# The last chunk of a gated recurrence gathered for the first expert in two one-pass parts

## The chip, the cores and the metric

The kernel runs on one core of one Trainium2 chip. The metric is device time in microseconds (us) of one execution; the profile is one execution taken by the hardware profiler. TensorE (PE) multiplies matrices, VectorE (DVE), ScalarE (ACT) and GpSimd (POOL) work on tiles, and SyncE (SP) issues DMAs.

## The reference

The program is a gated linear recurrence followed by a mixture of eight experts, one expert for each token.

```python
mag = sqrt(a_re*a_re + a_im*a_im); scale = minimum(mag, 0.999) / (mag + 1e-6)
for t in range(S):                          # B=4, H=8, S=768, D=48
    new_re = ar * S_re - ai * S_im          # ar, ai: the scaled gates of step t
    new_im = ar * S_im + ai * S_re
    S_re, S_im = new_re + k[t] outer v[t], new_im
    y[t] = q[t] @ S_re
x = y as 3072 tokens of 384
do_compute = x @ w_skip > 0                 # the others stay x
e = argmax(x @ w_gate); g = softmax(x @ w_gate)[e]
out = x + g * (maximum(x @ w1[e], 0) @ w2[e])   # w1: 8x384x1024, w2: 8x1024x384
```

## The kernel before, in words

**Tiling.** The 768 steps are cut into 6 chunks c of 128; a *unit* (c,b) is one chunk of one batch b, with all 8 heads. `unit()` runs for every unit: TensorE forms the scores `pa` (q times k, L635, 16 records in two halves), VectorE masks them into `at` (L657), and the output `py` is the sum of `at` times v (L705) and of the state `st` times q (L708). ScalarE copies `py` to `yT` (L710); TensorE multiplies `yT` with `wg` (L714), which gives `px`: the unit's 128 tokens with 384 features, and the logits of gate and skip. VectorE sums the logits (`lgs`, L719), ScalarE copies the features to `xa` (L722), and a DMA writes them to the output (L724).

**The state of late chunks.** For c = 4 and 5 (`last(c)`) the state is made without TensorE: `RX[:,0]` is the carried state `T` times the first factor, by 8 ScalarE activations, one for each head (L668); `RX[:,1]` is the same state with its halves swapped (`T2`, which a DMA brings, L641), times the second factor, on VectorE (L670); VectorE joins the two to `st` (L681). `RX`, `yT` and `T2` have one buffer each.

**Routing and gather.** `route1()` takes each late unit's logits to a one-hot of its expert (`oh`, L875), to the count of earlier tokens of that expert (`pr`, two small matmuls, L877 and L878), and in the last chunk to `ohx`, a one-hot over the 240 places of expert 0 (L889). GpSimd scatters every unit's tokens to a table `xs` in memory by indirect DMA (L778). Experts 1 to 7 read their tokens from that table. Expert 0 doesn't wait for the last chunk's scatter: `early()` (L734) reads the rows of the chunks before, and `tokens(0)` (L1002) adds the last chunk's by TensorE: `pt` = sum over the four batches of `xa` times `ohx`, and the early rows times the identity. These are float32 matmuls of 120 columns, 30 of them, which the trace shows as 60 records (two passes each). `pt` has two PSUM tiles, one for each half of the places; each is split to a rounded part `xh` (ScalarE, L1029) and a rest `xl` (VectorE, L1030).

**Experts.** Each takes 8 tiles `ph` (L1057, 9 one-pass matmuls of 240 columns each: high and low parts of tokens and weights), their ReLU on ScalarE and VectorE, and two tiles `po` (L1084 to L1086). The weights of expert 0 are split to `h` (ScalarE, L989) and `l` (VectorE, L990) beside the last units, with ScalarE's cast put right behind `yT` in its queue.

**Order.** A planner in Python writes the units, routes and weight pieces by priorities and costs, and a scheduler then sets the order on each engine; every engine takes its instructions strictly in that order. `issue_after(x)` holds an instruction back until x has its place in the queue.

Of the kernel before, what the change touches and what calls it, by code (L numbers as in the profile page):

```python
# [9 lines left out]
F32 = mybir.dt.float32  # L10
F32R = mybir.dt.float32r
BF16 = mybir.dt.bfloat16
I32 = mybir.dt.int32
AF = mybir.ActivationFunctionType
# [6 lines left out]
DM = H * D  # L21
# [91 lines left out]
class Kern:  # L113
# [530 lines left out]
    def unit(self, c, b):  # L644
# [18 lines left out]
        if c > 0:  # L663
            T = self.T[b]
            X = self.un.tile([96, 2, H, D], F32, name=f"RX_{nm}", tag="RX", bufs=1)
            if late:
                for h in range(H):
                    A.activation(X[:, 0, h], T[:, h], AF.Identity, scale=self.F[:, 0, b * H + h:b * H + h + 1])  # L668
                o.act(384, H)
                V.tensor_tensor(X[:, 1], self.T2.pop(b), Fb[:, 1].to_broadcast([96, H, D]), ALU.mult)  # L670
            else:
                with self.tc.issue_after(self.cins):
                    V.tensor_tensor(X, T.unsqueeze(1).to_broadcast([96, 2, H, D]), Fb.to_broadcast([96, 2, H, D]), ALU.mult)
# [29 lines left out]
        for hp in range(H // 2):  # L703
            for j in range(2):
                PE.matmul(py[j * 64:j * 64 + 64, hp], vt_[:, 2 * hp + j], at[:, 2 * hp + j], start=True, stop=(c == 0))  # L705
            if c > 0:
                for j in range(2):
                    PE.matmul(py[j * 64:j * 64 + 64, hp], Sb[:, 2 * hp + j], QT(2 * hp + j), start=False, stop=True)  # L708
        yT = self.un.tile([128, H // 2, C], F32, name=f"yT_{nm}", tag="yT", bufs=1)
# [10 lines left out]
        else:  # L720
            A.copy(self.lg[:, b], px[:, :, 2 * D:])
        A.copy(xa[:, 0:DM].rearrange("p (a k) -> p a k", k=2 * D), px[:, :, 0:2 * D])  # L722
        r = b * S + c * C
        nc.sync.dma_start(self.out[r:r + C], xa[:, 0:DM])  # L724
# [9 lines left out]
    def early(self):  # L734

        m = self.rt.tile([128, B * XW], F32, name="early", tag="xa", bufs=2)
        o = self.un.tile([128, H * 96], F32, name="ohx", tag="kt", bufs=1)
        nx = 2 * DM
        self.xe = m[0:TP, 0:nx].rearrange("p (t d) -> p t d", d=DM)
        self.ohx = [o[:, b * CAP:(b + 1) * CAP] for b in range(B - 1)] + [m[:, nx:nx + CAP]]  # L740
        self.early_ins = self.nc.sync.dma_start(self.xe, self.xs[0:CAP, 0:DM].rearrange("(t p) d -> p t d", p=TP)).ins

    def units(self, g):
# [3 lines left out]
        for cc in range(2):  # L747
# [5 lines left out]
            if not self.last(c):  # L753
                self.lg = self.rt.tile([128, B, H // 2, E + 1], F32, name=f"lg_{c}", tag="lg", bufs=2)
            self.xa = self.rt.tile([128, B, XW], F32, name=f"xa_{c}", tag="xa", bufs=2)
            self.nc.gpsimd.tensor_copy(self.xa[:, :, DM], self.tok[:, :, c])
            for b in range(B):
# [170 lines left out]
    def attention(self):  # L928
        with ExitStack() as ctx:
# [13 lines left out]
            self.scat = []  # L943
            self.pr_ins, self.T2, self.ain, self.QK, self.Ew, self.T, self.pa, self.W, self.ready, self.nats, self.kqt = [{} for _ in range(11)]
            self.cpos = self.gates_done = self.cons_done = self.routes_done = self.units_done = 0
# [55 lines left out]

    def tokens(self, e, xg, xp, pt_):  # L1002

# [3 lines left out]
        xl = xp.tile([128, KD, CAP], F32R, name=f"xl_{e}", tag="xl")  # L1007
        pts = [pt_.tile([128, KD, TP], F32, name=f"pt_{e}_{t}", tag="pt") for t in range(2)]
        ks = lambda k: slice(k * 128, (k + 1) * 128)
        ts = lambda t: slice(t * TP, (t + 1) * TP)  # L1010
        eye = self.ident[0:TP, 0:TP]
        if e:
            for t, pt in enumerate(pts):
                for k in range(KD):
                    with self.tc.issue_after(self.ph_ins):
                        self.pt_ins = PE.transpose(pt[:, k], xg[:, t, ks(k)], eye).ins
        else:


            pr = self.pr_ins  # L1020
            for i, (b, x) in enumerate(((0, pr[2]), (1, self.px_ins), (-1, self.px_ins), (2, pr[3]), (3, pr[3]))):
                with self.tc.issue_after(x):
                    for t, pt in enumerate(pts):
                        for k in range(KD):
                            l, r = ((self.xe[:, t, ks(k)], eye) if b < 0 else
                                    (self.xa[:, b, ks(k)], self.ohx[b][:, ts(t)]))
                            PE.matmul(pt[:, k], l, r, start=(i == 0 and k == 0), stop=True, skip_group_check=True)
        for t, pt in enumerate(pts):
            self.pins = (A.copy(xh[:, :, ts(t)], pt).ins,  # L1029
                         V.tensor_tensor(xl[:, :, ts(t)], pt, xh[:, :, ts(t)], ALU.subtract).ins)  # L1030
        return xh, xl

    def moe(self):
        nc = self.nc
        V, A, PE, G = nc.vector, nc.scalar, nc.tensor, nc.gpsimd
        with ExitStack() as ctx:
# [4 lines left out]
            got = {}  # L1041
            xh, xl = self.tokens(0, None, xp, pt_)
            for e in range(E):
# [32 lines left out]
                if e + 1 < E:  # L1076
                    xh, xl = self.tokens(e + 1, got[e + 1], xp, pt_)
                for t in range(2):
# [228 lines left out]
```

## Time and profile before

| | before |
|---|---|
| median of 3 runs | 519.48 us (519.21 to 523.06) |
| profiled execution: time, span | 520.63 us, 518.9 us |
| TensorE busy, mean granted clock | 415.0 us (80%), 0.891 |
| VectorE busy | 406.9 us (78%) |
| ScalarE busy | 316.3 us (61%) |
| GpSimd busy | 100.8 us (19%) |
| moved by DMA | 88.64 MB, 173 GB/s of memory traffic |

Busy shares are means over stages. The stages here are the chunks of the recurrence, up to about 365 us, and the experts, from the first `ph` on. In the page's picture of 40 slices TensorE's digits are mixed in the first 24 slices and 8 or 9 in the rest, so a change has to be read from the stage that it touches. [...]

### The profile page before, as it was taken

The numbers are of one execution on the slowest core, as the hardware profiler recorded it, in microseconds if no ns is written. First come the engines' busy times: TensorE is split into PE (matmuls) and PEld (weight loads), VectorE is DVE, ScalarE is ACT, GpSimd is POOL, SyncE is SP. The second block draws the span as 40 slices with busy tenths as digits, with TensorE's granted clock in tenths as the row PEclk, the third lists the DMA queues.
The fourth block names the chain that finished last, engine by engine and source line by source line (L and its number), as shares of the span: only waits on it lengthen the run. The fifth ranks groups of instructions, "written<-read, shape, count | busy, mean of one in ns | idle before, by whom it ended". The sixth has DMA issues, their size and how long they took to land. (4 is left out here: it accounts for less than half of the span.)

```text
span 518.9 us, 10077 instructions
## 1 busy us (share of the span) xinstructions
PE 415.0 (80%) x3221; PEld 360.2 (69%) x3221; DVE 406.9 (78%) x1111; ACT 316.3 (61%) x746; POOL 100.8 (19%) x174
## 2 busy tenths in 40 slices
PE   0336545499899313999999999998999999999993
PEld 0224323379777202688787888997899999999993
DVE  4999897989999999688878956888569668766730
ACT  5778777655557665568878665674266546554520
POOL 4002011111123454001000151321311111211111
PEclk9976666589999655699999999998999999999998
DMA  5557876589889887877755348764788668666300
GB/s 95 114 111 169 198 182 141 134 190 215 215 194 239 196 209 170 187 159 150 174 127 137 78 106 237 177 194 123 242 227 246 218 230 275 188 200 222 116 21 27
DMA packets 165218, 88.64 MB, mean 171 GB/s; under 512 B 138939, under 2 KB 158860, under 8 KB 165159
## 3 DMA queue, kind: packets, MB, share of 16 engines
q1 hardware_dynamic: 158135, 72.09, 55.2%
q0 software_dynamic: 5936, 15.65, 10.9%
q8 instruction: 28, 0.46, 0.4%
q10 hardware_dynamic: 1088, 0.20, 0.2%
q14 instruction: 31, 0.25, 0.2%
HBM read 63.19 MB, written 26.58 MB: 173 GB/s over the span
## 5 line engine op out<-in xcount | busy, mean ns | idle before, releaser
L496 PE MATMUL sw<-ws,ident 128*128 128x384 f32 x84 | 44.4, 665 | 34.5 <-ACT ws L482 34.5
L413 DVE TENSOR_TENSOR X<-W,ain 128x192 f32<-128x192 f32 x192 | 68.0, 354 | 3.5 <-ACT ain L339 0.2
L990 DVE TENSOR_TENSOR l<-r,h 128x768 fp32r<-128x768 f32 (+1 forms) x56 | 59.5, 1066 | 12.4 <-ACT h L989 12.2
L1059 ACT ACTIVATE hh<-ph 128x240 fp32r<-128x240 f32 x64 | 23.6, 374 | 58.1 <-PE ph L1057 58.0
L989 ACT CAST h<-r 128x768 fp32r<-128x768 f32 (+1 forms) x56 | 51.6, 928 | 5.3 <-DMA r<-in_moe_w_dram 4.9
L496 PEld LDWEIGHTS sw<-ws,ident 128*128 128x128 f32 x84 | 19.3, 254 | 47.0 <-ACT ws L482 37.3
L422 DVE TENSOR_TENSOR W<-X 128x96 f32<-128x96 f32 x192 | 49.0, 255 | 3.6
L1057 PE MATMUL ph<-xh,l 128*128 128x240 f32 x192 | 51.1, 275 | 0.0
L1057 PE MATMUL ph<-xh,h 128*128 128x240 f32 x192 | 49.7, 274 | 0.6 <-issue 0.6
L1057 PE MATMUL ph<-xl,h 128*128 128x240 f32 x192 | 49.3, 276 | 0.0
L578 PE MATMUL tp<-ident,iw 128*96 128x128 f32 x128 | 24.1, 339 | 29.5 <-DVE iw L514 24.9
L585 ACT COPY qk<-tp 96x256 f32<-96x256 f32 x128 | 39.8, 369 | 8.6 <-PE tp L578 8.3
L1084 PE MATMUL po<-h,hh 128*120 128x384 f32 x128 | 43.3, 338 | 0.0
L657 DVE TENSOR_TENSOR at<-pa,mask 128x512 f32<-128x512 f32 x48 | 32.5, 684 | 13.6 <-PE pa L635 11.5
L1085 PE MATMUL po<-l,hh 128*120 128x384 f32 x128 | 43.1, 337 | 0.0
L578 PEld LDWEIGHTS tp<-ident,iw 128*96 128x96 f32 x128 | 18.4, 158 | 34.0 <-issue 10.3
L705 PE MATMUL py<-at,vt 128*64 128x128 f32 x384 | 41.3, 287 | 0.0
L778 POOL DMA_INDIRECT xs<-xa,sl x24 | 28.6, 1193 | 64.2 <-DVE sl L845 19.9
L1086 PE MATMUL po<-h,hl 128*120 128x384 f32 x128 | 40.9, 341 | 0.0
L1060 DVE SCALAR_TENSOR_TENSOR hl<-ph,hh 128x240 fp32r<-128x240 f32 x64 | 25.6, 404 | 16.5 <-ACT hh L1059 16.0
L1090 POOL DMA_INDIRECT out_dram<-og,idx x16 | 19.3, 1209 | 87.5 <-DVE og L1089 49.2
L1057 PEld LDWEIGHTS ph<-xh,l 128*128 128x128 f32 x192 | 36.3, 189 | 0.0
(232 smaller groups left out, 1096.7 us busy)
## 6 DMA issues: line engine op xcount, KB each, us to landing
r<-in_moe_w_dram SPq DMA_DIRECT2D x24, 512.0 KB, 5.1
r<-in_moe_w_dram SPq DMA_DIRECT2D x32, 384.0 KB, 3.4
nat<-kq SPq DMA_DIRECT2D x8, 768.0 KB, 6.1
kq<-nw POOLq DMA_DIRECT2D x24, 192.0 KB, 3.7
kq<-iw POOLq DMA_DIRECT2D x24, 192.0 KB, 3.0
vt<-in_v_dram SPq DMA_DIRECT2D x24, 192.0 KB, 3.6
out_dram<-xa SPq DMA_DIRECT2D x24, 192.0 KB, 3.5
ain<-in_a_im_dram SPq DMA_DIRECT2D x90, 48.0 KB, 2.5
```

The source lines that it names most:

```text
L413: V.tensor_tensor(X, prev.unsqueeze(1).to_broadcast([128, 2, 2, D]), windows(ain[:, j]), ALU.mult)
L422: self.cins = V.tensor_tensor(W[:, j, ::-1], X[:, :, 0], X[:, :, 1], ALU.add).ins
L496: nc.tensor.matmul(sw, self.ident, ws[:, :, c], start=(c == 0), stop=(c == 1))
L578: nc.tensor.transpose(tp[:, jj], src[:, s * 4 + jj], self.ident)
L585: nc.scalar.copy(o, tp[:, :, :, cc].rearrange("p j s b -> p b s j"))
L705: PE.matmul(py[j * 64:j * 64 + 64, hp], vt_[:, 2 * hp + j], at[:, 2 * hp + j], start=True, stop=(c == 0))
L989: nc.scalar.copy(hi[:, ks], raw)
L990: nc.vector.tensor_tensor(lo[:, ks], raw, hi[:, ks], ALU.subtract)
L1057: pe = PE.matmul(ph, w[:, k, js], x[:, k], start=(n == 0), stop=(n == len(terms) - 1))
L1084: PE.matmul(po, hh[:, j, sl], w2h[:, j], start=(j == 0), stop=False)
L1085: PE.matmul(po, hh[:, j, sl], w2l[:, j], start=False, stop=False)
L1086: pe = PE.matmul(po, hl[:, j, sl], w2h[:, j], start=False, stop=(j == NF - 1))
```

## The change

For units of the last two chunks the 8 activations of `RX` now stand behind the previous unit's `yT` in ScalarE's queue. In the last chunk every unit's tokens are also written as a rounded part `hi` (ScalarE, 128x384, tile `xah`) and a rest `lo` = `xa` - `hi` (GpSimd, tile `xal`). The gather for expert 0 goes by thirds of the features, one PSUM bank for each (the third bank from the ring of `ph`): 24 one-pass matmuls of 240 columns (4 batches, 3 thirds, two parts), and 6 float32 matmuls of 120 columns for the early rows. Their places in TensorE's queue change, and the copies to `xh` and `xl` go by thirds: ScalarE, VectorE, ScalarE, and three subtractions on VectorE.

```diff
--- before.py
+++ after.py
@@ -664,8 +664,9 @@
             T = self.T[b]
             X = self.un.tile([96, 2, H, D], F32, name=f"RX_{nm}", tag="RX", bufs=1)
             if late:
-                for h in range(H):
-                    A.activation(X[:, 0, h], T[:, h], AF.Identity, scale=self.F[:, 0, b * H + h:b * H + h + 1])
+                with self.tc.issue_after(self.yT_ins):
+                    for h in range(H):
+                        A.activation(X[:, 0, h], T[:, h], AF.Identity, scale=self.F[:, 0, b * H + h:b * H + h + 1])
                 o.act(384, H)
                 V.tensor_tensor(X[:, 1], self.T2.pop(b), Fb[:, 1].to_broadcast([96, H, D]), ALU.mult)
             else:
@@ -705,7 +706,8 @@
                 PE.matmul(py[j * 64:j * 64 + 64, hp], vt_[:, 2 * hp + j], at[:, 2 * hp + j], start=True, stop=(c == 0))
             if c > 0:
                 for j in range(2):
-                    PE.matmul(py[j * 64:j * 64 + 64, hp], Sb[:, 2 * hp + j], QT(2 * hp + j), start=False, stop=True)
+                    self.py_ins[b] = PE.matmul(py[j * 64:j * 64 + 64, hp], Sb[:, 2 * hp + j], QT(2 * hp + j),
+                                               start=False, stop=True).ins
         yT = self.un.tile([128, H // 2, C], F32, name=f"yT_{nm}", tag="yT", bufs=1)
         self.yT_ins = A.copy(yT.rearrange("p a (k t) -> p a k t", k=2),
                              py.rearrange("p a (k t) -> p a k t", k=2)[:, :, :, ::-1]).ins
@@ -719,7 +721,13 @@
             V.tensor_reduce(lg, px[:, :, 2 * D:].rearrange("p h e -> p e h"), AX.X, ALU.add)
         else:
             A.copy(self.lg[:, b], px[:, :, 2 * D:])
+        if c == NCH - 1:
+            hi, lo = [t[:, b] for t in self.parts]
+            A.copy(hi.rearrange("p (a k) -> p a k", k=2 * D), px[:, :, 0:2 * D])
         A.copy(xa[:, 0:DM].rearrange("p (a k) -> p a k", k=2 * D), px[:, :, 0:2 * D])
+        if c == NCH - 1:
+            nc.gpsimd.tensor_tensor(lo, xa[:, 0:DM], hi, ALU.subtract)
+            o.act(384)
         r = b * S + c * C
         nc.sync.dma_start(self.out[r:r + C], xa[:, 0:DM])
         self.lg_t = o.act(1024, 3, o.pe(3000 if c else 2000))
@@ -734,10 +742,10 @@
     def early(self):
 
         m = self.rt.tile([128, B * XW], F32, name="early", tag="xa", bufs=2)
-        o = self.un.tile([128, H * 96], F32, name="ohx", tag="kt", bufs=1)
+        o = self.un.tile([128, B, CAP], F32R, name="ohx", tag="qkT")
         nx = 2 * DM
         self.xe = m[0:TP, 0:nx].rearrange("p (t d) -> p t d", d=DM)
-        self.ohx = [o[:, b * CAP:(b + 1) * CAP] for b in range(B - 1)] + [m[:, nx:nx + CAP]]
+        self.ohx = [o[:, b] for b in range(B)]
         self.early_ins = self.nc.sync.dma_start(self.xe, self.xs[0:CAP, 0:DM].rearrange("(t p) d -> p t d", p=TP)).ins
 
     def units(self, g):
@@ -753,6 +761,8 @@
             if not self.last(c):
                 self.lg = self.rt.tile([128, B, H // 2, E + 1], F32, name=f"lg_{c}", tag="lg", bufs=2)
             self.xa = self.rt.tile([128, B, XW], F32, name=f"xa_{c}", tag="xa", bufs=2)
+            if c == NCH - 1:
+                self.parts = [self.un.tile([128, B, DM], F32R, name=f"xa{k}", tag="nat") for k in "hl"]
             self.nc.gpsimd.tensor_copy(self.xa[:, :, DM], self.tok[:, :, c])
             for b in range(B):
 
@@ -999,35 +1009,43 @@
         self.fetch_ins = ld.ins
         return xg
 
-    def tokens(self, e, xg, xp, pt_):
+    def tokens(self, e, xg, xp, pt_, ph_):
 
         nc = self.nc
         V, A, PE = nc.vector, nc.scalar, nc.tensor
         xh = xp.tile([128, KD, CAP], F32R, name=f"xh_{e}", tag="xh")
         xl = xp.tile([128, KD, CAP], F32R, name=f"xl_{e}", tag="xl")
-        pts = [pt_.tile([128, KD, TP], F32, name=f"pt_{e}_{t}", tag="pt") for t in range(2)]
         ks = lambda k: slice(k * 128, (k + 1) * 128)
         ts = lambda t: slice(t * TP, (t + 1) * TP)
         eye = self.ident[0:TP, 0:TP]
         if e:
+            pts = [pt_.tile([128, KD, TP], F32, name=f"pt_{e}_{t}", tag="pt") for t in range(2)]
             for t, pt in enumerate(pts):
                 for k in range(KD):
                     with self.tc.issue_after(self.ph_ins):
                         self.pt_ins = PE.transpose(pt[:, k], xg[:, t, ks(k)], eye).ins
-        else:
-
-
-            pr = self.pr_ins
-            for i, (b, x) in enumerate(((0, pr[2]), (1, self.px_ins), (-1, self.px_ins), (2, pr[3]), (3, pr[3]))):
-                with self.tc.issue_after(x):
-                    for t, pt in enumerate(pts):
-                        for k in range(KD):
-                            l, r = ((self.xe[:, t, ks(k)], eye) if b < 0 else
-                                    (self.xa[:, b, ks(k)], self.ohx[b][:, ts(t)]))
-                            PE.matmul(pt[:, k], l, r, start=(i == 0 and k == 0), stop=True, skip_group_check=True)
-        for t, pt in enumerate(pts):
-            self.pins = (A.copy(xh[:, :, ts(t)], pt).ins,
-                         V.tensor_tensor(xl[:, :, ts(t)], pt, xh[:, :, ts(t)], ALU.subtract).ins)
+            for t, pt in enumerate(pts):
+                self.pins = (A.copy(xh[:, :, ts(t)], pt).ins,
+                             V.tensor_tensor(xl[:, :, ts(t)], pt, xh[:, :, ts(t)], ALU.subtract).ins)
+            return xh, xl
+
+        pts = [p.tile([128, CAP], F32, name=f"pt_{e}_{k}", tag=tag)
+               for k, (p, tag) in enumerate(((pt_, "pt"), (pt_, "pt"), (ph_, "ph")))]
+        px, pr = self.px_ins, self.pr_ins
+        for i, (b, x) in enumerate(((0, self.py_ins[2]), (1, px), (2, px), (-1, pr[3]), (3, pr[3]))):
+            with self.tc.issue_after(x):
+                for k, pt in enumerate(pts):
+                    if b < 0:
+                        for t in range(2):
+                            PE.matmul(pt[:, ts(t)], self.xe[:, t, ks(k)], eye, start=False, stop=True, skip_group_check=True)
+                        continue
+                    for n, xa in enumerate(self.parts):
+                        PE.matmul(pt, xa[:, b, ks(k)], self.ohx[b], start=(i + n == 0), stop=True, skip_group_check=True)
+        A.copy(xh[:, 0], pts[0])
+        V.tensor_copy(xh[:, 1], pts[1])
+        hi = A.copy(xh[:, 2], pts[2]).ins
+        for k, pt in enumerate(pts):
+            self.pins = hi, V.tensor_tensor(xl[:, k], pt, xh[:, k], ALU.subtract).ins
         return xh, xl
 
     def moe(self):
...
```

Up to about 325 us all queues are the same in both kernels, and from the first `ph` on they have the same order of work. Between these points three places matter. In the names the first number is the batch b, and the last a running number.

ScalarE's queue at units (5,0) to (5,2), before:

```order
L668 ACTIVATE RX_2_4328<-T_2_4008,F_4130 96x48 x4
L710 COPY yT_0_4196<-py_0_4179 128x512
L989 CAST h_0_4041<-r_0_2_4150 128x768
L668 ACTIVATE RX_2_4328<-T_2_4008,F_4130 96x48 x4
L881 ACTIVATE m_3_4314<-m_3_4314 128x8
L722 COPY xa_4145<-px_0_4198 128x384
L668 ACTIVATE RX_3_4413<-T_3_4100,F_4130 96x48 x8
L710 COPY yT_1_4283<-py_1_4266 128x512
```

and now:

```order
L712 COPY yT_0_4198<-py_0_4181 128x512
L999 CAST h_0_4041<-r_0_2_4152 128x768
L669 ACTIVATE RX_1_4245<-T_1_3923,F_4130 96x48 x8
L726 CAST xah<-px_0_4200 128x384
L727 COPY xa_4145<-px_0_4200 128x384
L891 ACTIVATE m_0_4407<-m_0_4407 128x8
L712 COPY yT_1_4287<-py_1_4270 128x512
L999 CAST h_0_4041<-r_0_4_4216 128x768
L669 ACTIVATE RX_2_4334<-T_2_4008,F_4130 96x48 x8
L726 CAST xah<-px_1_4289 128x384
L727 COPY xa_4145<-px_1_4289 128x384
L891 ACTIVATE m_1_4470<-m_1_4470 128x8
```

The activations of one unit's `RX` stood ahead of, around or (for `RX_3`) all in front of a `yT`; now all 8 stand behind the previous unit's `yT` and the weight cast, and the two copies of `px` behind them.

TensorE's queue where chunk 4 ends, from the last half of `py` of (4,3) in the first fence and from `pa` of (5,1) in the second; before:

```order
L705 MATMUL py_3_4102<-at_3_4038,vt_164 64x128 x2
L708 MATMUL py_3_4102<-qk_0_2167,st_166 64x128 x2
L705 MATMUL py_3_4102<-at_3_4038,vt_164 64x128 x2
L708 MATMUL py_3_4102<-qk_0_2167,st_166 64x128 x2
L877 LDWEIGHTS tri
L877 MATMUL pr_1_4140<-oh_1_4062,tri 128x8
L878 LDWEIGHTS ones
L878 MATMUL pr_1_4140<-ohs,ones 128x8
L635 MATMUL pa_1_0_4165<-qk_1_2168 128x128 x4
L635 MATMUL pa_1_1_4166<-qk_1_2168 128x128 x4
```

and now:

```order
L635 MATMUL pa_1_0_4167<-qk_1_2168 128x128 x4
L716 MATMUL px_2_4029<-wg,yT_2_4027 128x105 x4
L706 MATMUL py_3_4102<-at_3_4038,vt_164 64x128 x2
L635 MATMUL pa_1_1_4168<-qk_1_2168 128x128 x4
L709 MATMUL py_3_4102<-qk_0_2167,st_166 64x128 x2
L706 MATMUL py_3_4102<-at_3_4038,vt_164 64x128 x2
L709 MATMUL py_3_4102<-qk_0_2167,st_166 64x128 x2
L706 MATMUL py_3_4102<-at_3_4038,vt_164 64x128 x2
L709 MATMUL py_3_4102<-qk_0_2167,st_166 64x128 x2
L706 MATMUL py_3_4102<-at_3_4038,vt_164 64x128 x2
L709 MATMUL py_3_4102<-qk_0_2167,st_166 64x128 x2
```

Both halves of `pa` of (5,1) moved from behind `py` of (4,3) to places ahead of its state products (L708, now L709).

TensorE's queue at the end of the last chunk, from the `pr` of batch 2, before:

```order
L878 MATMUL pr_2_4503<-ohs,ones 128x8
L1027 MATMUL pt_0_4592<-ohx,xa_4145 128x120 x3
L1027 MATMUL pt_1_4593<-ohx,xa_4145 128x120 x3
L714 MATMUL px_3_4443<-wg,yT_3_4441 128x105 x4
L1027 MATMUL pt_0_4592<-ohx,xa_4145 128x120 x3
L1027 MATMUL pt_1_4593<-ohx,xa_4145 128x120 x3
L1027 MATMUL pt_0_4592<-ident,early 128x120 x3
L1027 MATMUL pt_1_4593<-ident,early 128x120 x3
L877 LDWEIGHTS tri
L877 MATMUL pr_3_4532<-oh_3_4520,tri 128x8
L878 LDWEIGHTS ones
L878 MATMUL pr_3_4532<-ohs,ones 128x8
```

and now, the last 4 of the 14 products that stand between `px_3` and `pr_3`, and what follows:

```order
L1043 MATMUL pt_1_4603<-ohx,xah 128x240
L1043 MATMUL pt_1_4603<-ohx,xal 128x240
L1043 MATMUL pt_2_4604<-ohx,xah 128x240
L1043 MATMUL pt_2_4604<-ohx,xal 128x240
L887 LDWEIGHTS tri
L887 MATMUL pr_3_4542<-oh_3_4530,tri 128x8
L888 LDWEIGHTS ones
L888 MATMUL pr_3_4542<-ohs,ones 128x8
L1040 MATMUL pt_0_4602<-ident,early 128x120 x2
L1040 MATMUL pt_1_4603<-ident,early 128x120 x2
L1040 MATMUL pt_2_4604<-ident,early 128x120 x2
L1043 MATMUL pt_0_4602<-ohx,xah 128x240
```

Before, batch 0 stood ahead of `px_3`, batch 1 and the early rows between `px_3` and `pr_3`, batches 2 and 3 behind. Now no product of the gather stands ahead of `px_3` (but 4 of batch 0 behind `py_2`), 14 short products stand between, and 12 records of early rows and 6 products of batch 3 behind.

## Rows read from the trace of the kernel before

**Rows 1.** Busy time by window: length, busy per engine (instructions), PEclk, DMA share, GB/s
```profile
350.00:355.00 5.00, 4.35 (x54) 3.91 (x54) 5.00 (x26) 2.46 (x11) 1.26 (x2) 1.00 0.61 187
355.00:360.00 5.00, 3.80 (x36) 3.61 (x37) 4.94 (x31) 2.66 (x8) 0.97 (x1) 0.76 0.37 87
375.00:380.00 5.00, 5.00 (x41) 5.00 (x40) 1.49 (x4) 2.09 (x5) 0.00 (x0) 1.00 0.75 179
400.00:440.00 40.00, 40.00 (x298) 40.00 (x296) 28.98 (x47) 22.53 (x42) 6.77 (x8) 1.00 0.75 242
```

**Rows 2.** ScalarE timeline, 343 to 366 us: start, duration, instruction, idle before and releaser
```profile
343.83 0.56 ACT L710 COPY yT<-py 128x512 f32<-128x512 f32 x1
...
348.60 0.56 ACT L710 COPY yT<-py 128x512 f32<-128x512 f32 x1
349.07 0.83 ACT L989 CAST h<-r 128x768 fp32r<-128x768 f32 x1
349.80 1.01 ACT L668 ACTIVATE RX<-T,F 96x48 f32<-96x48 f32 x4
...
353.95 1.91 ACT L668 ACTIVATE RX<-T,F 96x48 f32<-96x48 f32 x8
355.77 0.56 ACT L710 COPY yT<-py 128x512 f32<-128x512 f32 x1
...
361.09 0.59 ACT L710 COPY yT<-py 128x512 f32<-128x512 f32 x1 [1.81 <-PE py L708]
...
364.88 0.59 ACT L710 COPY yT<-py 128x512 f32<-128x512 f32 x1 [0.47 <-PE py L708]
```

**Rows 3.** TensorE timeline, 355 to 365 us, same columns
```profile
355.45 0.17 PE L877 MATMUL pr<-oh,tri 128*128 128x8 bf16 x1 [1.09 <-DVE oh L875]
...
356.39 1.14 PE L714 MATMUL px<-wg,yT 128*128 128x105 f32 x8 [0.75 <-ACT yT L710]
...
357.79 0.65 PE L708 MATMUL py<-qk,st 96*64 96x128 f32 x4
...
360.35 0.65 PE L708 MATMUL py<-qk,st 96*64 96x128 f32 x4
...
363.06 0.39 PE L708 MATMUL py<-qk,st 96*64 96x128 f32 x4
...
364.39 0.39 PE L708 MATMUL py<-qk,st 96*64 96x128 f32 x4
```

**Rows 4.** TensorE timeline at 342.6 us, the scores of one unit
```profile
342.61 2.03 PE L635 MATMUL pa<-qk 96*128 96x128 f32 x16
```

**Rows 5.** VectorE timeline, 349 to 371 us, same columns
```profile
349.86 0.55 DVE L670 TENSOR_TENSOR RX<-T,F 96x384 f32<-96x384 f32 x1 [2.01 <-DMA T<-T]
...
356.30 0.60 DVE L681 SCALAR_TENSOR_TENSOR st<-RX,sg 96x384 f32<-96x384 f32 x1
...
368.71 0.23 DVE L875 SCALAR_TENSOR_TENSOR oh<-iota,m 128x8 bf16<-128x8 f32 x1
...
370.80 0.34 DVE L889 TENSOR_SCALAR early<-iotac,m 128x240 f32<-128x240 bf16 x1
```

**Rows 6.** TensorE timeline, 365 to 376 us, end of recurrence to first expert
```profile
365.33 1.58 PE L1027 MATMUL pt<-ohx,xa 128*128 128x120 f32 x12
366.74 1.04 PE L714 MATMUL px<-wg,yT 128*128 128x105 f32 x8
...
371.79 1.50 PE L1027 MATMUL pt<-early,xa 128*128 128x120 f32 x12
373.88 0.35 PE L1057 MATMUL ph<-xh,h 128*128 128x240 f32 x1 [0.60 <-issue]
...
375.98 1.17 PE L1057 MATMUL ph<-xl,h 128*128 128x240 f32 x9
```

**Rows 7.** GpSimd by line: shapes, count, busy and mean ns, idle before
```profile
L199 POOL CAST iotac<-ii 128x240 bf16<-128x240 int32 x1 | 0.4, 372 | 0.0
...
L201 POOL MEMSET zrow<- 128x386 f32 x1 | 0.4, 410 | 0.0
```

More of the change, by code (lines that the diff above doesn't have):

```diff
@@ L943, in attention @@
             self.scat = []
-            self.pr_ins, self.T2, self.ain, self.QK, self.Ew, self.T, self.pa, self.W, self.ready, self.nats, self.kqt = [{} for _ in range(11)]
+            self.pr_ins, self.py_ins, self.T2, self.ain, self.QK, self.Ew, self.T, self.pa, self.W, self.ready, self.nats, self.kqt = [{} for _ in range(12)]
             self.cpos = self.gates_done = self.cons_done = self.routes_done = self.units_done = 0
@@ L1041, in moe @@
             got = {}
-            xh, xl = self.tokens(0, None, xp, pt_)
+            xh, xl = self.tokens(0, None, xp, pt_, ph_)
             for e in range(E):
@@ L1076, in moe @@
                 if e + 1 < E:
-                    xh, xl = self.tokens(e + 1, got[e + 1], xp, pt_)
+                    xh, xl = self.tokens(e + 1, got[e + 1], xp, pt_, ph_)
                 for t in range(2):
```

## The prediction

> **What bounds the kernel now.** I read the busy time by windows first, to see which stage is limited by what. In the first expert and in the middle of the experts TensorE is busy 5.00 of 5.00 and 40.00 of 40.00 us at a granted clock of 1.00 [rows 1]. Whatever moves the first `ph` (373.88 us, [rows 6]) therefore moves the end by as much, and nothing that the other engines do behind it counts. At 350 to 360 us it is otherwise: TensorE is busy 4.35 and 3.80 of 5.00, VectorE 5.00 and 4.94, and the clock falls to 0.76 in the second window [rows 1]. So the question is what sets the time from chunk 4's end to the first `ph`.
>
> The second view is the timeline of ScalarE and TensorE in that stretch. The five `yT` from (4,3) to (5,3) start at 343.83, 348.60, 355.77, 361.09 and 364.88 us [rows 2]: steps of 4.77, 7.17, 5.32 and 3.79 us, 21.05 in all. The third is late because the 8 activations of `RX_3` stood in front of it, 1.91 us from 353.95 [rows 2]. [...] From the last `yT` to the first `ph` 9.00 us pass (364.88 to 373.88): 12 records of batch 0 stand ahead of `px_3` and the others around and behind `pr_3` [rows 6].
>
> **The change, part by part.**
>
> *Scores ahead of `py`.* The 16 records of `pa` of (5,1) now stand in front of (4,3)'s state products. They take (2.03 - 0.28) / 15 x 16 = 1.87 us [rows 4], 0.28 being about one record's length. Before, they started when `py` of (4,3) was done, at 342.61, and that unit's `yT` waited for ScalarE until 343.83 [rows 2, 4]. Now `py` ends at 342.61 + 1.87 = 344.48 and `yT` starts 0.1 later, at 344.6: +0.8 us. If TensorE comes to this point earlier, it is 0; that is the lower bound.
>
> *The activations behind `yT`.* This makes the last chunk one serial loop, `yT`, weight cast, `RX`, `st`, state products, `yT`. Its steps: `yT` to cast 0.47 (348.60 to 349.07), cast to `RX` 0.73 (349.07 to 349.80), 8 activations 1.91 [rows 2]; `st` 0.60 [rows 5]; the state part of `py` at full clock 1.72 (363.06 to 364.39 + 0.39), and 0.10 from its end to `yT` (364.78 to 364.88) [rows 2, 3]. The sum is 5.53. Two handovers, `RX` to `st` and `st` to `py`, are in no row; the nearest is that 0.10 from TensorE to ScalarE, the lower bound is 0, and where VectorE is busy they can be longer. I take 0.10 each, so 5.73 us for a round, and four rounds 22.9 us against 21.05. The last `yT` starts at 344.6 + 22.9 = 367.5 us, 2.6 later than before.
>
> What lies beside the loop: the other half of the state, which waited 2.01 us for the DMA of `T` [rows 5], has a round of 5.73 us in place of some 4; the two copies of `px` to `hi` and `xa`, each no longer than a `yT` of more columns (0.59, [rows 2]), end some 4.3 us behind `yT` and leave ScalarE over 1 us before the next. If that cover were gone, the second copy's 0.5 us would be added to a round. VectorE worked 9.94 us for the about two units of 350 to 360 us [rows 1], some 5 of 5.73 us for a round, so it can delay `st` by some tenths; that is in the upper bound, 5.9 us.
>
> *The gather.* A 240-column product should come every 0.112 us, like those of `ph` ((1.17 - 0.28) / 8, [rows 6]), and a record of 120 columns every 0.111 ((1.50 - 0.28) / 11, [rows 6]). So 60 records become 24 + 12 = 36, and TensorE has 24 x 0.111 = 2.7 us less to do. Only what stands between the last `yT` and the first `ph` counts. From the start Y of that `yT`: `px_3` starts at Y + 0.62 (355.77 to 356.39, [rows 2, 3]), takes 1.04 [rows 6] and ends at Y + 1.7. From there to the end of `oh` it is 1.16 us (367.78 to 368.94, [rows 5, 6]), so `pr_3` could go at Y + 2.9; the 14 products in front of it take 1.57 us and end at Y + 3.2. Then 12 records of early rows (1.33) to Y + 4.6, and 6 products of batch 3 (0.67) to Y + 5.3. The one-hot of batch 3 takes 0.34 [rows 5] and a few small steps behind `pr_3`, and is there by Y + 4.2. Before, 0.59 us passed from the gather's end (371.79 + 1.50) to the first `ph`, for the copy to `xh`; now the first third's copy starts four products before the gather ends, and 0.2 of it is left. First `ph`: Y + 5.5. That is 3.5 us less than 9.00.
>
> *The subtraction on GpSimd.* No row shows one. `zrow`'s fill of 128x386 takes 0.41 us, and a conversion of 128x240 takes 0.37 [rows 7], which for 384 columns and two inputs is 0.37 x 1.6 x 2 = 1.2; I take 1.2, since it has two inputs. For batch 3 `xa` ends at about Y + 2.7 and `lo` is first used at Y + 4.7, so 2.0 us are covered and this costs nothing; one of 3 us would cost 1. [...] The scatter of batch 3 stands behind the subtraction on GpSimd's queue and moves with it; only expert 1 waits for that, some 10 us later.
>
> **The sum.** First `ph` at 367.5 + 5.5 = 373.0 us against 373.88: -0.9 us at full clock. The bounds: a round of 5.53 and no +0.8 gives 343.83 + 22.1 + 5.5 = 371.4, -2.4; a round of 5.9 gives 373.7, -0.2. To this comes the clock. One `py` at half clock cost 361.00 - 357.79 = 3.21 against 1.72 us, +1.5 [rows 3]. Before, it fell when TensorE had waited 1.09 + 0.75 us within 2 us. In the new rounds of (5,2) and (5,3) there are no scores left to fill: `py`, `px`, `pr` and four products make some 3.5 us of a round of 5.73, and 2.2 us are waits for `yT` and `st`. I expect the clock to fall once more, for one `py`: -0.9 + 1.5 = +0.6.
>
> The sum stands against the profiled execution, 520.63 us with a span of 518.9, which is 1.15 above the median of 519.48. I put the difference on the median: 520.1 us.
>
> **Rivals.**
> *Full clock (chance 0.2).* No `py` falls into a slow stretch, because the waits are spread in pieces and TensorE has work between them. Against it: before, smaller waits were enough [rows 3]. -0.9: 518.6 us.
> *Two slow rounds, the slower side (0.27).* [...] -0.9 + 3.0 = +2.1: 521.6 us. It decides as soon as the clock does not come back in (5,2)'s `py`, as it did before. For it: both waits return each round. Against it: in the profile the clock came back after one `py`. [...] If the half clock also held through the tail (3.6 us of records from `px_3`'s end), it would be +5.7: 525.2 us; I give that 0.05 of the 0.27.
> *A late part (0.07).* `lo` over 2.0 us, or the weight cast waiting for its DMA with all 8 activations now behind that cast on ScalarE. A wait of 1 us on top of the forecast: 521.1 us.
> *The loop does not form (0.06).* The queue says that `RX` is behind `yT`, but if its cost was hidden before and stays hidden, rounds keep their 21.05 us: 344.6 + 21.05 + 5.5 = 371.2, -2.7 and 516.8 us. Against it is the sum of 5.53 us, which has no slack in it.
> The forecast, one slow `py`, has the remaining 0.4.
>
> **The numbers.** The predicted time is 520.1 us. The range goes from 517.2 (full clock with a round between 5.53 and 5.73) to 523.0 us (two slow rounds with a round of 5.9 and a late part of 0.7); it leaves out the loop that doesn't form and the half clock through the tail. A measurement of this kernel can tell about 1%, 5.2 us, from no change. Of the cases only the half clock through the tail is beyond that, 0.05, and a little for what I have not seen on either side: faster 0.03, same 0.91, slower 0.06.
>
> **What would show it.** In the profile after: steps between the `yT` of chunk 5 of 5.6 to 5.9 us, and one about 1.5 longer; `RX` starting 1.2 us behind each `yT`; VectorE's `st` right behind the eighth activation. 14 products at 0.11 us between `px_3` and `pr_3`, and a first `ph` 5.5 us behind the last `yT`, at 373 to 375 us. `xal` at 0.4 to 1.2 us, with TensorE not waiting for it. The window of (5,2) with a granted clock below 1.00. I am wrong if a one-pass product of the gather takes longer than one of `ph`, if `st` waits for VectorE's other work, or if the clock stays at either level through all of the last two units.

## The result, and the profile after

The changed kernel is slower: 522.54 us median of 14 runs (519.77 to 524.92) against 516.27 for the kernel before in as many runs beside it (513.65 to 523.06); the ratio is 1.0113, with a 95% interval of 1.0082 to 1.0144. Some executions fall in a slower state; ratios are of the others alone, medians and ranges of all, so the two differ a little. The forecast time of 520.1 us and its range hold the median. The forecast difference, +0.6 us, does not hold: the measured one is +5.8 us by the ratio (1.13% of 516.27) and +6.3 by the medians, over the 1% to which I gave a chance of 0.06. The three runs of before that the forecast was put on (519.21 to 523.06) lie above ten of the eleven later ones.

Where the time went is read from one stretch, from the start of the `yT` of (4,0) to the first `ph`. In front of it the queues are the same but for a few instructions, yet the starts differ: over the 13 profiles of this study that `yT` starts between 318.1 and 325.4 us, with granted clocks of 0.82 to 0.97 at 200 to 250 us. Behind it TensorE is busy all the time (40.00 of 40 us at 400 to 440 us in both): from the first `ph` to the start of the last `po` it is 136.26 us before and 136.33 after. In the stretch it is 49.13 us before and 55.88 after, +6.75: chunk 4 takes 1.39 more, the four rounds of chunk 5 take 27.29 against 21.05, and the tail, from the `yT` of (5,3) to the first `ph`, 8.12 against 9.00.

ScalarE's timeline of the changed kernel, which answers to [rows 2] (start, duration, instruction, idle before):

```profile
341.95 0.59 ACT L712 COPY yT<-py 128x512 f32<-128x512 f32 x1 [0.94 <-PE py L709]
...
347.74 0.58 ACT L712 COPY yT<-py 128x512 f32<-128x512 f32 x1 [2.20 <-PE py L709]
...
353.50 0.58 ACT L712 COPY yT<-py 128x512 f32<-128x512 f32 x1 [1.78 <-PE py L709]
...
360.55 0.59 ACT L712 COPY yT<-py 128x512 f32<-128x512 f32 x1 [3.04 <-PE py L709]
...
361.77 1.91 ACT L669 ACTIVATE RX<-T,F 96x48 f32<-96x48 f32 x8
...
369.24 0.58 ACT L712 COPY yT<-py 128x512 f32<-128x512 f32 x1 [3.47 <-PE py L709]
```

Rounds of 5.79, 5.76, 7.05 and 8.69 us; every `yT` now waits for TensorE, none for an `RX`. TensorE's timeline, which answers to [rows 3, 6]:

```profile
354.13 1.14 PE L716 MATMUL px<-wg,yT 128*128 128x105 f32 x8 [0.60 <-ACT yT L712]
...
357.73 0.44 PE L709 MATMUL py<-qk,st 96*64 96x128 f32 x4 [2.08 <-DVE st L682]
...
359.38 0.65 PE L706 MATMUL py<-at,vt 128*64 128x128 f32 x4
...
365.89 0.69 PE L709 MATMUL py<-qk,st 96*64 96x128 f32 x4 [2.78 <-DVE st L682]
...
368.50 0.64 PE L709 MATMUL py<-qk,st 96*64 96x128 f32 x4
...
372.59 0.41 PE L1043 MATMUL pt<-ohx,xah 128*128 128x240 f32 x1
372.81 0.41 PE L1043 MATMUL pt<-ohx,xal 128*128 128x240 f32 x1
...
374.85 1.83 PE L1040 MATMUL pt<-ident,early 120*128 120x120 f32 x12
...
377.36 0.38 PE L1075 MATMUL ph<-xh,h 128*128 128x240 f32 x1
```

In (5,2) TensorE waits 0.60 us for `yT` and 2.08 for `st`, in (5,3) 2.78 for `st`; four records of `py` then take 0.65 us, as in the slow `py` of before [rows 3]. The products of the gather come every 0.21 us, at half clock (0.50 granted at 370 to 375 us), until the clock comes back in the early rows. The windows, which answer to [rows 1] and have the same columns (start and end, length, busy time of PE, PEld, DVE, ACT and POOL, granted clock, DMA share, GB/s):

```profile
355.00:360.00 5.00, 2.92 (x33) 2.57 (x33) 3.88 (x21) 2.52 (x11) 0.12 (x1) 0.83 0.63 165
360.00:365.00 5.00, 3.10 (x24) 2.35 (x20) 3.24 (x12) 3.32 (x11) 1.99 (x3) 0.83 0.07 25
365.00:370.00 5.00, 3.52 (x31) 3.10 (x31) 3.04 (x17) 1.36 (x4) 1.90 (x2) 0.52 0.72 212
370.00:375.00 5.00, 5.00 (x25) 4.92 (x26) 2.59 (x15) 0.97 (x3) 1.85 (x2) 0.50 0.78 299
375.00:380.00 5.00, 5.00 (x41) 4.81 (x42) 2.44 (x13) 1.14 (x4) 1.00 (x1) 0.96 0.10 25
400.00:440.00 40.00, 40.00 (x298) 39.99 (x297) 29.59 (x47) 22.01 (x40) 7.59 (x7) 1.00 0.73 230
```

TensorE is busy 2.92 and 3.10 of 5 us in the windows in which the clock begins to fall. Windows of 2 us show that it falls twice:

```profile
356.00:358.00 2.00, 0.28 (x5) 0.28 (x7) 2.00 (x12) 1.51 (x6) 0.00 (x0) 1.00 0.22 25
358.00:360.00 2.00, 2.00 (x26) 2.00 (x24) 0.88 (x7) 0.00 (x0) 0.00 (x0) 0.58 0.89 270
...
362.00:364.00 2.00, 1.10 (x11) 0.76 (x10) 1.97 (x5) 1.68 (x8) 1.01 (x2) 1.00 0.14 49
364.00:366.00 2.00, 0.11 (x2) 0.11 (x4) 1.93 (x11) 0.97 (x3) 1.11 (x2) 0.79 0.00 0
366.00:368.00 2.00, 2.00 (x20) 2.00 (x22) 1.43 (x6) 0.00 (x0) 0.91 (x1) 0.50 0.69 216
```

It falls behind a window with 0.28 of 2 us busy, is back at 1.00 at 362 to 364 us, and falls again around one with 0.11 busy; then it stays at 0.50 through `py` of (5,3), `px` and the 14 products. The experts run at 1.00 as before (400 to 440 us). VectorE and GpSimd beside the wait for the second `st`, which answers to [rows 5, 7]:

```profile
361.69 0.15 DVE L897 SCALAR_TENSOR_TENSOR m<-oh,pr 128x1 f32<-128x1 bf16 x1 [2.78 <-PE pr L888]
...
361.84 1.23 DVE L903 TENSOR_TENSOR ohs<-ohs,oh 128x8 bf16<-128x8 bf16 x1
...
363.51 0.96 DVE L1000 TENSOR_TENSOR l<-r,h 128x768 fp32r<-128x768 f32 x1
...
365.22 0.61 DVE L682 SCALAR_TENSOR_TENSOR st<-RX,sg 96x384 f32<-96x384 f32 x1
...
365.94 1.01 DVE L885 SCALAR_TENSOR_TENSOR oh<-iota,m 128x8 bf16<-128x8 f32 x1
```

```profile
362.17 0.88 POOL L729 TENSOR_TENSOR xal<-xa,xah 128x384 fp32r<-128x384 f32 x1
...
365.88 1.03 POOL L729 TENSOR_TENSOR xal<-xa,xah 128x384 fp32r<-128x384 f32 x1
```

`ohs`, 8 columns, takes 1.23 us and ends with GpSimd's subtraction at 363.05; `oh` takes 1.01 and ends with the next one. `RX` was ready at 363.68 (361.77 + 1.91), but `st` comes at 365.22, behind batch 1's route and the weights' `l` in VectorE's queue. VectorE itself had stood idle for 2.78 us until the `pr` of batch 1 came (361.40), which stands behind the slow `py` of (5,2) and four products of the gather in TensorE's queue: part of TensorE's wait for `st` goes back to its own slow work.

### The profile page after: what moved, and what is told of

Its sections match the earlier page's. It is cut to its first block, busy times and chain, and to the rows that moved or that the text cites. A ratio compares the mean times of both kernels' runs of the same rounds, so it can differ in the third digit from the quotient of the medians.

```text
span 522.0 us, 10028 instructions
## 1 busy us (share of the span) xinstructions
PE 415.7 (80%) x3197; PEld 359.0 (69%) x3197; DVE 410.8 (79%) x1113; ACT 316.5 (61%) x750; POOL 102.2 (20%) x178
## 5 line engine op out<-in xcount | busy, mean ns | idle before, releaser
L788 POOL DMA_INDIRECT xs<-xa,sl x24 | 26.6, 1108 | 65.9 <-DVE sl L855 20.0
L635 PE MATMUL pa<-qk 96*128 96x128 f32 x256 | 35.5, 286 | 3.3 <-DVE at L657 2.9
L635 PEld LDWEIGHTS pa<-qk 96*128 96x128 f32 x256 | 31.4, 194 | 7.5 <-DVE at L657 4.1
```

The source lines that it names most:

```text
L635: nc.tensor.matmul(pa[h // 4][:, h % 4], KT(h), QT(h), start=True, stop=True)
```

## The experiments

Stretch and parts in us, each from one profile; the ratio is to the kernel before, in runs beside it.

| kernel | (4,0) to (4,3) | rounds of chunk 5 | tail | stretch | ratio (95%) |
|---|---|---|---|---|---|
| before | 19.08 | 4.77, 7.17, 5.32, 3.79 | 9.00 | 49.13 | |
| before, again | 19.31 | 4.77, 6.79, 6.36, 5.50 | 9.00 | 51.73 | |
| changed | 20.47 | 5.79, 5.76, 7.05, 8.69 | 8.12 | 55.88 | 1.0113 (1.0082 to 1.0144) |
| changed, again | 20.47 | 5.78, 5.75, 6.99, 7.41 | 5.64 | 52.04 | 1.0107 (1.0039 to 1.0175) |
| hold alone | 20.47 | 5.78, 5.76, 7.18, 7.49 | 9.56 | 56.24 | 1.0140 (1.0080 to 1.0199) |
| gather alone | 19.25 | 4.78, 6.99, 5.73, 3.79 | 8.00 | 48.54 | 1.0034 (0.9996 to 1.0073) |
| changed, `lo` on VectorE | 20.46 | 5.79, 5.75, 7.22, 7.73 | 7.70 | 54.65 | 1.0134 (1.0075 to 1.0193) |
| gather, `lo` on VectorE | 19.24 | 4.77, 7.05, 6.37, 3.96 | 6.47 | 47.86 | 0.9989 (0.9947 to 1.0031) |
| changed, waits filled | 20.46 | 5.79, 5.75, 6.31, 6.36 | 5.53 | 50.20 | 1.0060 (1.0025 to 1.0095) |
| changed, cast behind `RX` | 20.47 | 5.75, 6.24, 6.78, 6.51 | 5.53 | 51.28 | 1.0034 (0.9995 to 1.0073) |
| hold two back | 18.08 | 4.82, 5.36, 5.49, 3.77 | 8.75 | 46.27 | 0.9991 (0.9951 to 1.0030) |
| two back, gather | 18.70 | 4.53, 6.04, 5.04, 3.81 | 6.43 | 44.55 | 0.9994 (0.9957 to 1.0031) |
| the same, casts behind ReLU | 18.38 | 4.55, 5.64, 5.05, 3.81 | 6.44 | 43.87 | 0.9950 (0.9924 to 0.9976) |

**The two halves of the change.** Hold alone, in the kernel before:

```diff
-                for h in range(H):
-                    A.activation(X[:, 0, h], T[:, h], ...)
+                with self.tc.issue_after(self.yT_ins):
+                    for h in range(H):
+                        A.activation(X[:, 0, h], T[:, h], ...)
```

> The kernel before with one edit only: the RX activations of late units held behind the previous unit's yT. Theory L: the loop forms, rounds of about 5.8 us and two slower ones at half clock, the last yT at 368 to 370 us, and the old gather of 9 us behind it, longer at half clock: first ph at 377 to 381 us, 520 to 524 us in all (before 516.3). Rival G: holding is harmless, within 1.5 us of the kernel before.

Measured: ratio 1.0140; stretch 56.24. The time of the changed kernel is there without any of the gather, and so are the waits for `st` (1.68 and 0.84 us) and the half clock:

```profile
350.00:355.00 5.00, 2.72 (x32) 2.11 (x30) 4.51 (x21) 3.60 (x12) 0.59 (x1) 0.92 0.66 165
355.00:360.00 5.00, 4.41 (x36) 3.99 (x35) 2.38 (x15) 1.89 (x5) 0.97 (x1) 0.50 0.20 67
360.00:365.00 5.00, 4.16 (x34) 3.57 (x35) 2.38 (x14) 1.79 (x8) 1.24 (x1) 0.50 0.53 173
```

The gather alone is the changed kernel with these lines taken back.

> The changed kernel with the RX activations given back their old freedom in ScalarE's queue (no holding behind yT); the two-part gather, GpSimd's subtraction and the new batch places stay. Theory L (the loop): holding RX behind yT makes chunk 5 a serial loop of 5.8 us a round and starves TensorE of work, which brings the half clock; the gather itself is a gain. Then the last yT should start near 365 us again (before 364.88, changed 369.24) and the first ph some 5.5 to 6.5 us behind it, at about 371 us: 2 to 3.5 us under the kernel before, about 513 to 514.5 us against its 516.3. Rival G (the gather's own parts): GpSimd's subtraction holds VectorE up and the gather products in front of pr delay the routes; then this kernel stays near the changed one, 520 us or more, with the last yT after 367 us.

Measured: 1.0034 (0.9996 to 1.0073): not slow as the changed kernel, but not the gain that I expected either. Its last `yT` starts where it should (362.25 in a profile that began 3.0 us earlier), and its tail is 8.00, not 5.5 to 6.5. VectorE, GpSimd and TensorE in that tail:

```profile
362.61 1.77 DVE L898 TENSOR_SCALAR ohx<-iotac,m 128x240 fp32r<-128x240 bf16 x1
...
367.10 1.55 DVE L902 TENSOR_TENSOR ohs<-ohs,oh 128x8 bf16<-128x8 bf16 x1
```

```profile
363.20 1.03 POOL L728 TENSOR_TENSOR xal<-xa,xah 128x384 fp32r<-128x384 f32 x1
...
367.75 0.88 POOL L728 TENSOR_TENSOR xal<-xa,xah 128x384 fp32r<-128x384 f32 x1
```

```profile
366.64 0.17 PE L886 MATMUL pr<-oh,tri 128*128 128x8 bf16 x1 [0.59 <-DVE m L916]
...
369.12 0.57 PE L1042 MATMUL pt<-ohx,xah 128*128 128x240 f32 x3 [0.85 <-DVE m L914]
```

A one-hot of 240 columns takes 1.77 us and `ohs` 1.55, where they take 0.33 and 0.15 elsewhere; each ends within 0.2 us of a subtraction's end (364.23 and 368.63). Both begin some 0.6 us ahead of the subtraction's recorded start, beside the scatter that GpSimd issues before it; but beside such an issue alone, in the kernel before, the same one-hot takes 0.33 (358.68, issue from 358.55 to 359.52) and `ohs` 0.15 (365.69, issue from 365.39 to 366.40). TensorE waits 0.59 and 0.85 us for that chain. Both theories were half right here.

**The subtraction on VectorE**, first in the changed kernel, then in the gather alone:

```diff
-            nc.gpsimd.tensor_tensor(lo, xa[:, 0:DM], hi, ALU.subtract)
+            V.tensor_tensor(lo, xa[:, 0:DM], hi, ALU.subtract)
```

> The changed kernel with the rest lo = xa - hi made by VectorE in place of GpSimd; all else is as changed. In the changed kernel's trace four VectorE instructions beside GpSimd's subtractions took 0.59, 1.23, 1.01 and 0.75 us where they take 0.15 to 0.23 elsewhere. Theory L: they cost about 1 us on the path to st of unit (5,3) and little else, so this kernel is 0 to 1.5 us faster than the changed one (521 to 522.5 us), with the same rounds of 5.8 us. Rival G: the stalls are the cause, and it falls to 518 us or less.

Measured: 1.0134 against 1.0113: no difference is shown. `st` of (5,3) came sooner, 7.73 in place of 8.69, but the clock was 0.50 from 360 to 375 us, so little was left of it.

> Both edits: RX not held, and lo made by VectorE. Theory L: like the gather alone, 512.5 to 514.5 us, at most 1 us faster than with GpSimd's subtraction, since VectorE has four subtractions of some 0.5 us more. Rival G: only this one is faster than the kernel before, and the gather alone is not.

Measured: 0.9989; the tail 6.47 where GpSimd's subtraction had 8.00. In the changed kernel with `lo` on VectorE a subtraction takes 0.54 to 0.56 us, and with none on GpSimd `ohs` takes 0.15 to 0.16, `oh` 0.21 to 0.22 and `ohx` 0.34 us. The expected gain of some 3 us over before would be a ratio of 0.994, just outside the interval's edge (0.9947): it is not there.

**The clock.** TensorE gets work to do in the waits of (5,2) and (5,3), without use. If the clock falls because TensorE waits there, it should stay at 1.00 now and the stretch be shorter in spite of the work; if the fall has another cause, it should be 0.50 again and the stretch no shorter.

```diff
+            if c == NCH - 1 and b > 1 and hp == 0:
+                for j in 7 * (0, 1):
+                    PE.matmul(py[j * 64:j * 64 + 64, hp], vt_[:, 2 * hp + j], at[:, 2 * hp + j], start=True, stop=True)
             for j in range(2):
                 PE.matmul(py[j * 64:j * 64 + 64, hp], ...
```

> The changed kernel with work added: in units (5,2) and (5,3) the first two products of py are written seven times more before they are written for good, 14 float32 products (28 records of 0.055 us, some 1.6 us) in front of the products that wait for st. The outputs are the same. [...]

Measured: with work added the kernel is not slower than the changed one but rather faster, 1.0060 against 1.0113 with intervals that overlap a little; the stretch is 50.20. Windows, and TensorE in (5,2):

```profile
350.00:355.00 5.00, 3.68 (x51) 3.27 (x52) 4.89 (x24) 4.09 (x13) 0.03 (x1) 1.00 0.63 155
355.00:360.00 5.00, 4.95 (x70) 4.40 (x66) 3.60 (x19) 3.29 (x11) 1.95 (x3) 1.00 0.16 59
360.00:365.00 5.00, 3.58 (x46) 3.22 (x45) 3.87 (x22) 1.57 (x5) 2.73 (x3) 1.00 0.67 206
365.00:370.00 5.00, 5.00 (x46) 4.78 (x45) 4.01 (x22) 1.51 (x5) 2.04 (x3) 1.00 0.89 328
```

```profile
351.81 1.75 PE L707 MATMUL py<-at,vt 128*64 128x128 f32 x28
353.39 0.39 PE L709 MATMUL py<-at,vt 128*64 128x128 f32 x4
354.56 0.44 PE L712 MATMUL py<-qk,st 96*64 96x128 f32 x4 [0.78 <-DVE st L682]
```

28 added records in 1.75 us leave 0.78 of the wait; the clock stays at 1.00 in this profile, and the tail is 5.53 us, with the same queue behind `px_3` that took 8.12. The rounds at full clock are 6.3 us and not 5.73: `st` is still late behind VectorE's queue. (The profile is of this kernel's shortest execution, 514.37 us where the median is 519.02; its stretch began at 318.11 us, the earliest of all 13.)

**The cast out of the loop**: the weight cast is pinned behind the last `RX` activation, not behind `yT`.

```diff
...
-                    for x in self.pins if e else (self.yT_ins, self.at_ins):
+                    for x in self.pins if e else (self.rx_ins, self.at_ins):
```

> The changed kernel with one move: the weight cast of a unit stands behind the RX activations on ScalarE, not between yT and RX; TensorE's queue is the same but for one place of one pr. Theory L: the cast is a link of the loop, 0.73 us of each round, so the first two rounds of chunk 5 take 5.0 to 5.1 us in place of 5.79 and 5.76, and the stretch from yT of (4,0) to the first ph is about 3 us shorter, 52 to 53.5 us. Rival H (rounds are set by VectorE or TensorE): rounds stay at 5.6 us or more.

Measured: 1.0034, some 4 us faster than the changed kernel; but the first two rounds are 5.75 and 6.24, as the rival has it. There `st` isn't what TensorE waits for:

```profile
346.37 1.16 PE L635 MATMUL pa<-qk 96*128 96x128 f32 x8 [0.44 <-DVE at L657]
...
352.12 1.16 PE L635 MATMUL pa<-qk 96*128 96x128 f32 x8 [0.57 <-DVE at L657]
```

The scores `pa` wait for the mask step, which frees their bank, and these scores stand in front of the state products. So it seems that two loops of about the same length lay on each other. The gain came in the last two rounds, 13.29 us against 15.74 and 14.40, where no scores are left. (This profile is of its longest execution, 522.77 us where the median is 517.73; its stretch began at 325.43, the latest of all 13.)

**Holding two units back.** The activations stand behind the `yT` of b-2, so that no state waits for the previous one, and no `yT` stands behind all 8 of them.

```diff
+                with self.tc.issue_after(self.yT_prev):
...
+        self.yT_prev = getattr(self, "yT_ins", None)
         self.yT_ins = A.copy(...
```

> The kernel before with the RX activations held behind the yT of two units earlier, not of the previous one: RX of (5,3) then stands behind yT of (5,1), but one round earlier than in the changed kernel, so no state waits for the previous yT. Theory L (what costs is the serial loop, not that RX stands behind a yT): yT of (5,1) starts near 352.5 us, not 355.77, TensorE gets px and py of (5,2) 2 to 3 us earlier, and from the yT of (4,0) to the first ph it takes 45 to 47 us (before 49.1, holding one back 56.2): 2 to 4 us faster than the kernel before. Rival H (any hold behind yT costs): 53 us or more from yT of (4,0) to the first ph, as with holding alone.

> The hold of two units back together with the two-part gather and lo made by VectorE. Theory L: both gains add, last yT as with the hold of two back, then a tail of about 6.5 us as with the gather and VectorE (before 9.0): 42.5 to 45 us from yT of (4,0) to the first ph, 4 to 6 us faster than the kernel before in all. Rival H: no faster than the gather with VectorE alone (47.9 us in that stretch).

Measured: stretches of 46.27 and 44.55, as expected, at a clock of 1.00 in every window from 330 to 380 us; but ratios of 0.9991 and 0.9994. Part is given back behind the first `ph`: 137.38 and 137.74 us from there to the last `po`, where all others but the last kernel have 136.0 to 136.4. That is 1.1 to 1.5 us of the 4 to 6 by which these stretches lie under the mean of the two of the kernel before (50.43); where the rest of the gain went isn't shown. ScalarE and TensorE in the second one:

```profile
380.34 0.84 ACT L1000 CAST h<-r 128x768 fp32r<-128x768 f32 x1 [4.19 <-DMA r<-in_moe_w_dram]
...
383.16 0.36 ACT L1078 ACTIVATE hh<-ph 128x240 fp32r<-128x240 f32 x1
```

```profile
383.58 0.44 PE L1103 MATMUL po<-h,hh 128*120 128x384 f32 x1 [0.88 <-ACT hh L1078]
```

The first expert ends sooner than expert 1's weights arrive; a cast waits 4.19 us for them, and the ReLU that the last `po` needs stands behind three such casts. The last kernel puts these casts behind that ReLU: the first four pieces of expert 1's weights come at j = 3, the others at j = 7.

```diff
-                    if e == 0 and j == 3:
+                    if e == 0 and j in (3, 7):
                         self.pins = hs
...
```

> The hold of two units back, the two-part gather and lo on VectorE, and one more move: the last three weight casts of expert 1 stand behind the ReLU of expert 0's last ph on ScalarE, not in front of it. In the kernel without that move TensorE waited 0.88 us for that ReLU behind a cast that waited 4.19 us for its DMA, and from the first ph to the last po it took 137.7 us against 136.3. Theory L: 136.3 to 136.7 us from the first ph on, 44.5 us in the stretch before it, in all 1 to 1.5 us faster than without the move and 3 to 4.5 us faster than the kernel before, a ratio of 0.991 to 0.995. Rival D (weights arrive too late by DMA whatever the order): 137.5 us or more from the first ph, a wait for weights in its place.

Measured: 0.9950 (0.9924 to 0.9976), 515.36 us: faster than both kernels of the change. From the first `ph` it takes 137.22 us, which is neither theory's figure: half a microsecond came back and not 1 to 1.5. The wait of 0.88 is gone, but TensorE is still idle for 0.6 us between 375 and 395 us.

**Again.** The changed kernel and the kernel before, unaltered.

> The changed kernel unaltered, for a second profile beside the others: is the half clock through the tail a habit of it or of one execution? Theory C (the waits of the last two rounds bring it each time): again 0.5 to 0.6 between the state products of (5,2) and the early rows, 54.5 to 57 us from the yT of (4,0) to the first ph. Rival N (chance of one execution): the clock stays near 1.00 there and the stretch is 50 to 52 us.

> The kernel before unaltered, for a second profile. From the yT of (4,0) to the first ph 48 to 50 us as in the first one (49.1), with at most one py at half clock; if this stretch differed by several us between executions, the comparisons by stretch would be worth less than they are taken for here.

Measured: 1.0107 for the changed one. Its second profile has the slow rounds again (0.66 at 365 to 370 us) but not the slow tail: 5.64. The kernel before has a slow stretch of its own this time, 51.73:

```profile
350.00:355.00 5.00, 5.00 (x37) 4.82 (x38) 4.02 (x23) 1.26 (x3) 1.15 (x1) 0.50 0.16 51
355.00:360.00 5.00, 4.26 (x30) 3.67 (x30) 2.43 (x15) 2.11 (x5) 0.97 (x1) 0.50 0.39 113
```

Here `py` of (5,2) and the first half of that of (5,3) run at half clock without any hold. So one kernel's stretch moves by 2.6 to 3.8 us between executions, with the clock. The mean of the two pairs is +3.5 us (53.96 against 50.43); with two executions of each it can't be told from the +5.8 of the ratio, and the rest I can't place.

## Why the prediction was right and wrong

- *The time, 520.1 us*: inside its range partly by luck. The runs that it was put on had a median 3.2 us above that of all 14 (519.48 against 516.27), and the difference was forecast 5.7 us too small by the medians; the two errors go against each other.
- *TensorE sets the end from the first `ph` on*: right, for this change. For the larger gain of the hold two back it is not (137.38 and 137.74 us): expert 1's weights come too late.
- *Scores ahead of `py`, +0.8*: the measured term is +1.2 to +1.4 (20.47 with the hold, 19.08 to 19.31 without). The direction was right; what the other half microsecond is isn't shown. TensorE is busy 5.00 of 5 us from 330 to 340 us there.
- *The loop, 5.73 us a round*: 5.79 and 5.76 in the first two rounds, but partly by luck, since the loop of masks and scores seems to be as long there (TensorE waits 0.44 and 0.43 us for the masks, and the cast moved out left 5.75). In the last two it is the loop through `st`, and 6.3 us at full clock: the term was 0.6 too small, because VectorE's queue has batch 1's route and `l` in front of `st`. I had that as "some tenths", within 5.9; and `st` waiting for VectorE's other work, which I named as a sign of being wrong, is what the trace shows.
- *The clock, +1.5 once*: this is the step that failed. Before, one `py` was slow [rows 3], with a granted clock of 0.50 at 358 to 360 us and 1.00 again at 362 to 364, and I took one again. Both `py` were slow, wholly or for the most part, in each of the five profiles with the hold of one unit and without the fill, and in one of the two profiles of the changed kernel the tail was, too. Against the kernel with the waits filled, whose clock stayed at 1.00, the last two rounds and the tail are 5.7 us longer in one profile of the changed kernel (23.86 against 18.20) and 1.8 in the other (20.04). The rival of two slow rounds (0.27) is what happened. That its worst case, +5.7 us (0.05), lies close to the measured +5.8 is partly luck: the tail was slow in one of the two profiles and lost 2.6 us there, not 3.6, and late `st` made up for it. The argument for the rival was in my own working, 2.2 us of waits in each of the two rounds, and I weighed it less than the single fall of before. That single fall was one execution's: in the second profile of the kernel before a second `py` is half slow, so a second slow round is not the hold's alone.
- *The gather, 3.5 us off the tail*: right to a tenth at full clock and with the hold of one unit: 5.53 in two kernels for 5.5. Without it, with `lo` on VectorE, the tail is 6.43 to 6.47, also at full clock. In the changed kernel the half clock took 2.6 of it back in one profile.
- *The subtraction at no cost*: its own time was in the bounds (0.86 to 1.03 us for 0.41 to 1.2; the doubling for two inputs in the 1.2 was my estimate) and TensorE never waited for `lo`. But I looked only for who waits for its result. It holds VectorE, 0.4 to 1.5 us a piece, and costs 1.5 us of the tail in the gather alone (8.00 against 6.47, one profile each). There `ohs`, with two inputs, went from 0.15 to 1.55 us, and `ohx`, a TENSOR_SCALAR, from 0.33 to 1.77; by what the subtraction holds them, no run here shows.
- *Rivals.* "The loop does not form" is out: it forms in every kernel with the hold of one unit. "Full clock" is out in all of these but the filled one.

## What to carry to other kernels

Before an instruction is held behind another in a queue, ask which stage runs one step ahead because it isn't: here the state of the next unit was ready early, and a hold behind the `yT` of one unit back, not of two, made a serial loop of the chunk. Here the clock fell behind windows of 2 us with 0.28 us of work and around one with 0.11, and both `py` ran slow in five profiles: where a change opens such waits in a stage of short bursts, price the half clock for every burst behind the waits, not for one. Filling the waits with work without use tells whether it is the clock: here it stayed at 1.00. Take a second profile of both kernels before a slow burst is put down to the change. For work moved to GpSimd ask also what VectorE does meanwhile: here an `ohs` of 0.15 us took 1.55.

## What the runs showed that I had not expected

Some VectorE instructions of 1 to 240 columns are held to the end of a GpSimd subtraction of 128x384: 1.77 us in place of 0.33 (240 columns), 1.55 in place of 0.15 (8), and 0.75 in place of 0.16 (1, in the changed kernel). And 28 useless records a unit, 1.75 us of TensorE each, kept the clock at 1.00 in the profile taken and made the changed kernel, if anything, faster (1.0060 against 1.0113; the intervals overlap between 1.0082 and 1.0095).
